# Products of x with w_ch moved between the last group's chunks, and three weight loads cut unevenly

## The chip, the cores and the metric

The kernel runs on one core of a Trainium2 chip. The time is the device time of one execution in microseconds (us). Before the change it is 436.24 us, the median of three runs (435.94 to 436.3 us).

A core has five engines that run beside each other: TensorE (PE: matrix products; PEld is its loading of weights), VectorE (DVE), ScalarE (ACT), GpSimd (POOL) and SyncE (SP). PE writes only to the accumulation memory PSUM, which DVE and ACT read. Sixteen DMA engines move data between the main memory and the on-chip memory.

## The reference

Two layers follow one another. The first is a causal attention with 8 batches, 8 heads, 576 positions and 64 columns a head, and a bias from running sums of `s`. Its result, with the heads side by side, is `x` (8 x 576 x 512). The second mixes along the positions by frequency:

```python
X = np.fft.rfft(x, axis=1)
Xr, Xi = np.real(X[:, :64]), np.imag(X[:, :64])
Yr = einsum('bmd,mde->bme', Xr, w_r) - einsum('bmd,mde->bme', Xi, w_i)
Yi = einsum('bmd,mde->bme', Xr, w_i) + einsum('bmd,mde->bme', Xi, w_r)
y = np.fft.irfft(Y, n=576, axis=1)
u = x + y
out = u + np.maximum(u @ w_ch, 0.0)
```

`w_r` and `w_i` hold a 512 x 512 matrix for each of 64 frequencies: 134 MB in 32-bit numbers, which are read once.

## The kernel before

**Attention.** 32 steps `n` go through 4 groups `g` of two heads and 8 batches. A step computes scores, exponentials and the product with v, leaves its part of `x` in `x_all`, and transforms it to 64 frequencies. The frequency weights of the first three groups (a group is 128 rows of every matrix) are used in between by `quads`, as soon as a group's `x` is complete.

**The weight stream.** Nearly all loads are started by POOL from one list of transfers, by `load` (L311, the start is L315). The weights are asked for in "quarters": `loads_w(upto)` (L294) hands out those up to number `upto`. A unit `u` (`unit_loads`, L249) is 16 frequencies of `w_r` (even `u`) or `w_i` (odd `u`) for one group; there are 24 units of four quarters. A quarter goes to 32 partitions, each of which gets 16 KB of 16-bit numbers (512 KB in all, converted on the way from 1 MB). The last group's weights come as 16 tiles of two transfers each (`tile_loads`, L270): chunk `c` (8 frequencies) has a tile of `w_r` and then one of `w_i`; the last tile comes in four transfers of half size. How far step `n` asks is `on_chip[n]` (L337), a line in `n` that `fits` (L326) cuts where a buffer is still in use. Eight semaphores go round over POOL's transfers, so that the start of one waits until the eighth before it has landed.

**The last group.** After the attention, `modes(NG - 1, c)` (L619) multiplies chunk `c` of the last group: eight matmuls for `w_r`, eight for `w_i` (L628), then POOL's loads that its buffers allow (L645), then an addition of the sum over the other groups on DVE (L651), which gives `yb`. With a `meanwhile`, other work is put in PE's order ahead of one of its four parts (0 and 1 are `w_r`, 2 and 3 `w_i`). `y_transposed` (L839) transposes `yb` on PE (L842) and copies it on ACT (L844). `gather_round` (L857) multiplies transposed chunks with `w_ch` and brings them in order by frequency (L865); its copies (L876) are 16 of 64 rows for chunks 0 to 3 and 16 of 32 rows for chunks 4 and 5, half on ACT and half on DVE.

**Kept products.** The products of `x` with `w_ch` need no frequencies. `work()` (L882) transposes the next pair of blocks of `x` (`x_transposed`, L803: 8 matmuls at L809, two DVE copies at L813) and multiplies the pair before it with `w_ch` (`keep`, L827: 8 matmuls at L822, two ACT copies at L684). Ten calls deal with nine pairs. A tenth pair, `late[-1]`, goes by hand. Pairs 0 and 1 start their product early (`x_times_wch(0, False)`, `x_times_wch(1, False)`) and leave it in PSUM, where the frequency part is added later.

**The order around the change** (L990 to L1049) is Python that is unrolled: each engine carries out its instructions in that order. `TAKE` says how many calls of `work()` chunk `c` gets, `AHEAD` that chunks 0 to 2 may be multiplied one ahead. After chunk 5 stand the transposes of `late[-1]`, 0 and 1, the product of pair 0 and the second round of gathers; chunk 6 has `keep(late[-1])` between its `w_r` and `w_i`; chunk 7 has `first_z(1)` ahead of part 2 and `first_u` ahead of part 3. SP starts a two-number transfer `mark` (L1036) that waits for the last weights, and behind it the transfers `spread` (L662). Then a written list of steps (L1095) ends the work: products, sums and the stores of the result.

Of the kernel before, what the change touches and what calls it, by code (L numbers as in the profile page):

```python
# [19 lines left out]
def kernel(  # L20
# [12 lines left out]
    B, H, S, D = q.shape  # L33
    NM = moe_w_r.shape[0]
    DM = H * D
# [5 lines left out]
    NG = DM // P  # L41
# [6 lines left out]
    NCK = NM // MC  # L48
# [177 lines left out]
    HU = WM * DM  # L226
# [12 lines left out]
    def parts_of(u):  # L239
# [4 lines left out]
            return [(0, ya[:, HU:]), (3, xg[:, 4 * HU : 5 * HU])]  # L244
        return [(0, slot(UNIT_AT[u], 0, 4))]

    wt = {}

    def unit_loads(u):  # L249

        g, c, ri = u // NCK, u % NCK // 2, u % 2
        src = (moe_w_r, moe_w_i)[ri][:, g * P : (g + 1) * P, :]
        slots, todo = [], []
        for j0, t in parts_of(u):
            slots += [t[:, i : i + HU].rearrange("p (q e) -> p q e", q=QD) for i in range(0, t.shape[1], HU)]
        for h in range(QD):
            todo.append([])
            for j0, t in parts_of(u):
                first = 1 if ri == 1 and c + h + j0 == 0 else 0
                j1 = j0 + t.shape[1] // HU  # L260
                todo[-1].append((
                    t[QP * h : QP * h + QP, first * HU :].rearrange("p (j x) -> p j x", x=HU),
                    src[16 * c + 4 * (j0 + first) + h : 16 * c + 4 * j1 - 3 + h : 4].rearrange(
                        "j (p q) e -> p j (q e)", q=QD
                    ),
                ))
        wt[g, c, ri] = slots
        return todo

    def tile_loads(k):  # L270
# [23 lines left out]
    def loads_w(upto):  # L294
        todo = []
        while asked[0] < min(upto, NLW):
            if not queued:
                t = asked[0]
                queued.extend(unit_loads(t // 4) if t < 4 * NUN else tile_loads((t - 4 * NUN) // 2))
            todo += queued.pop(0)  # L300
            asked[0] += 1
        return todo

# [34 lines left out]
    for n in range(N):  # L338
        if n < B:
            w = 4 + (4 * NU + 2) * (n + 1) // (B + 1)  # L340
        else:
            w = 3 * n + 2 if n < 2 * B + 4 else max(59, 4 * n - 22)
        on_chip.append(fits(w, used[n]))


# [273 lines left out]
    def modes(g, c, meanwhile=None, ris=(0, 1)):  # L619


        ps = auxpool.tile([P, DM], FP32, name="yp", tag="aux")
        cols = spectrum(g).rearrange("p q x b m -> p q (x b) m")

        def product(ri, q_, cg):
            k0 = HP if ri == 1 and c == 0 and cg == 0 else 0
            c0 = 2 * B * (1 - ri)
            nc.tensor.matmul(  # L628
                ps[32 * cg : 32 * cg + 32, :],
                cols[k0:, q_, c0 : c0 + 4 * B, 8 * (c // 2) + 2 * cg + c % 2],  # L630
                wt[g, c, ri][cg // 2][k0:, 2 * (cg % 2) + q_, :],
                start=(ri == ris[0] and q_ == 0), stop=(ri == ris[-1] and q_ == 1),
                tile_position=(k0, 32 * cg), skip_group_check=True,
            )

        for x in range(2 * ris[0], 2 * ris[-1] + 2):
            ri, y = divmod(x, 2)
            if meanwhile and x in meanwhile:
                meanwhile[x]()
            for z in range(4):  # L640
                if meanwhile:
                    product(ri, z // 2, 2 * y + z % 2)
                else:
                    product(ri, y, z)
        load(loads_w(fits(NLW, 2 * NUN + 2 * c + ris[-1] + 1)))  # L645
        if ris[-1] == 0:
            nc.vector.tensor_tensor(out=y_acc[:, c, :], in0=ps, in1=y_acc[:, c, :], op=ALU.add)
            return None
        yb = fpool.tile([P, DM], FP16, name="y_sb", tag="y")
        for cols in halves if c == NCK - 1 else [slice(0, DM)]:  # L650
            nc.vector.tensor_tensor(  # L651
                out=yb[:, cols], in0=ps[:, cols], in1=y_acc[:, c, cols], op=ALU.add
            )
        if c >= NCK - 1:
            spread(c, 0, yb)
        return yb
# [146 lines left out]
    def x_transposed(i):  # L803
        xts[i] = xt_sb[len(xts) % 3]
        for x, (b, T) in enumerate(pairs[i]):
            ps = upool.tile([P, DT, P], FP32, name="xt_ps", tag="u")
            for rows, bb, ident in parts(b, T):
                for dt in range(DT):
                    nc.tensor.matmul(  # L809
                        ps[:, dt, rows], x_all[: rows.stop - rows.start, dt, bb, T, :],  # L810
                        ident, start=True, stop=True, skip_group_check=True,
                    )
            nc.vector.tensor_copy(out=xts[i][:, x], in_=ps)  # L813
# [25 lines left out]
    def y_transposed(yb, c=NCK):  # L839
        ps = auxpool.tile([P, DT, P], FP16, name="yt_ps", tag="aux")  # L840
        for dt in range(DT):
            nc.tensor.transpose(ps[:, dt, :], yb[:, bass.ts(dt, P)], ident16h)  # L842
        yt = yt_first[:, :, c % NY, :] if c < NCK - 2 else spool.tile([P, DT, P], FP16, name="yt_sb", tag="yt")
        nc.scalar.copy(out=yt, in_=ps)  # L844
        return yt
# [47 lines left out]

    late = [i for i in kept if i not in first_pairs]
    order_z = late[:-1]
    TAKE = (2, 2, 3, 0, 0, 0)
    us, rs = {}, {}
    last = len(pairs) - 1
    x_pool = ()
# [87 lines left out]
    def z_of(i):  # L987
        return [zs[i, x] for x in range(2)]

    AHEAD = 3  # L990
    ybs = {}
    work()
    for c in range(NCK - 2):
        for x in (c, c + 1):
            if x not in ybs and (x == c or x < AHEAD):
                ybs[x] = modes(NG - 1, x)
        yb = ybs[c]
        for x in range(TAKE[c] - 1):
            work()
        if c == NCK - 3:  # L1000
            x_transposed(late[-1])
            x_transposed(0)
        yt = y_transposed(yb, c)
        if TAKE[c]:
            work()
        if c >= NY:
            if c == NCK - 3:
                x_times_wch(0, False)
                x_transposed(1)
                for which, pool in ((1, auxpool), (0, upool)):  # L1010
                    for x in range(2):
                        gather_round(NY, NCK - 2, 4 * x, which, pool)("sv"[x])
        elif c == NY - 1:
            modes(NG - 1, NY, ris=(0,))
            for x, pool in enumerate((auxpool, upool, auxpool, auxpool)):
                if x == 2:
                    ybs[NY] = modes(NG - 1, NY, ris=(1,))
                for which in (1, 0):
                    gather_round(0, NY, 2 * x, which, pool)()
                if x >= 2:  # L1020
                    work()
    assert not order_z and not ahead
    c = NCK - 2
    yb6 = modes(NG - 1, c, {2: lambda: keep(late[-1])})
    x_times_wch(1, False, (0,))
    yt = y_transposed(yb6)
    x_times_wch(1, False, (1,))
    vb6 = y_times_wch(c, yt)


    def first_u():
# [107 lines left out]
```

## Time and profile before

| what | value |
|---|---|
| profiled execution, its own time | 437.91 us |
| its span, first to last instruction | 436.1 us |
| median of three runs | 436.24 us |
| PE, DVE, ACT, POOL busy | 87%, 59%, 57%, 31% of the span |
| moved by DMA | 92.87 MB as written, 213 GB/s in the mean |
| last weights landed | 400.12 us |
| last product of the last chunk (L628) | starts at 401.61 us, takes 0.65 us |

The profiled execution took 1.67 us more than the median of the runs, and its span 0.14 us less. Times "at" below are from the span's start. "Busy" of PE is modelled for matmuls that overlap. The line `DMA` of the 40 slices is the mean busy share of the sixteen engines; `PEclk` is the granted clock of TensorE. A row of the timeline gives start, duration, engine, line, operation, names and shape, the number of merged instructions, and in brackets the idle time before them and what ended it.

### The profile page before, as it was taken

The page shows a single profiled execution, that of the slowest core. Times are in us where ns is not written, and L with a number is a line of the kernel's source. Part 1 is how long each engine was busy: PE and PEld are TensorE (multiplying, and loading weights), DVE is VectorE, ACT ScalarE, POOL GpSimd, SP SyncE. Part 2 cuts the span into 40 slices and gives each one's busy share as a digit, 9 for nine tenths or more (in the row PEclk, how much of TensorE's full clock was granted, in tenths as well). Part 3 has the DMA queues.
Part 4 walks back from the last instruction along what each step waited for, and adds up shares of the span by engine and source line. Part 5 has one row for each costly group of instructions (what it writes and reads, how often), then busy time and mean ns, then how long its engine had stood idle before and what let it go on. Part 6 is the DMA issues. An engine that isn't in the chain of part 4 may idle for free. (4 is left out here: it accounts for less than half of the span.)

```text
span 436.1 us, 12627 instructions
## 1 busy us (share of the span) xinstructions
PE 381.2 (87%) x5395; PEld 220.2 (50%) x5395; DVE 256.8 (59%) x574; ACT 249.3 (57%) x556; POOL 136.4 (31%) x218
## 2 busy tenths in 40 slices
PE   1599999989999999999997889969885797788994
PEld 1256666645666655656654445535552354443441
DVE  7555666537766765677565566634643255563795
ACT  1377777725866855767774446536540243451894
POOL 6463243131333222323322222222222222210582
PEclk9999999999999999999999799999998799989998
DMA  8999999999999999999999999999999999994598
GB/s 161 208 210 209 213 207 208 213 214 211 212 208 211 210 210 214 210 211 207 210 210 214 212 211 213 210 214 214 212 210 211 212 211 211 211 208 84 202 366 323
DMA packets 47105, 92.87 MB, mean 213 GB/s; under 512 B 8222, under 2 KB 17946, under 8 KB 47050
## 3 DMA queue, kind: packets, MB, share of 16 engines
q0 software_dynamic: 40400, 81.28, 99.1%
q1 hardware_dynamic: 6650, 10.80, 7.1%
q8 instruction: 42, 0.69, 0.6%
q14 instruction: 13, 0.11, 0.1%
HBM read 163.29 MB, written 9.51 MB: 396 GB/s over the span
## 5 line engine op out<-in xcount | busy, mean ns | idle before, releaser
L513 ACT ACTIVATE p_sb<-sc_ps,cumt_sb 128x320 f16<-128x320 f32 (+1 forms) x384 | 161.0, 519 | 33.6 <-PE sc_ps L504 33.6
L504 PE MATMUL sc_ps<-qt,kt 128*64 128x256 bf16 (+3 forms) x640 | 95.4, 294 | 2.0 <-ACT kt L458 1.4
L504 PEld LDWEIGHTS <-kt 128*128 128x128 bf16 (+1 forms) x640 | 50.5, 126 | 62.7 <-issue 36.1
L315 POOL DMA_DIRECT2D w_sb<-in_moe_w_i_dram x62 | 35.2, 567 | 90.7 <-DMA w_sb<-in_moe_w_r_dram 36.5
L458 DVE COPY qt<-tr_ps 64x576 bf16<-64x576 bf16 x64 | 47.7, 745 | 19.6 <-PE tr_ps L454 19.3
L315 POOL DMA_DIRECT2D w_sb<-in_moe_w_r_dram x60 | 34.0, 567 | 76.8 <-DMA w_sb<-in_moe_w_r_dram 28.3
L550 DVE RECIPROCAL rcp<-av_ps 128x5 f32<-128x5 f32 x64 | 12.4, 193 | 75.9 <-PE av_ps L545 75.8
L493 PE MATMUL sc_ps<-negm,ident 128*128 128x512 bf16 x128 | 51.4, 401 | 0.0
L475 ACT ACTIVATE p<-sc_ps,cumt 128x64 f16<-128x64 f32 x32 | 10.1, 314 | 57.3 <-PE sc_ps L471 57.3
L545 PEld LDWEIGHTS <-p_sb 128*128 128x128 f16 x1088 | 40.4, 98 | 3.5
L454 PE MATMUL tr_ps<-ident,qk 64*64 64x64 bf16 x1152 | 31.6, 198 | 10.9 <-DVE kt L458 5.2
L458 ACT COPY kt<-tr_ps 64x576 bf16<-64x576 bf16 x32 | 22.9, 716 | 23.5 <-DVE qt L458 22.9
L454 PEld LDWEIGHTS <-qk 64*64 64x64 bf16 x1152 | 24.2, 111 | 23.7 <-DVE kt L458 8.3
L496 PE MATMUL sc_ps<-negm,ident 128*128 128x256 bf16 x128 | 36.1, 282 | 0.0
L605 PE MATMUL yp<-w_sb,xs 64*32 64x512 bf16 (+1 forms) x704 | 30.6, 403 | 5.0 <-DMA w_sb<-in_moe_w_i_dram 2.4
L545 PE MATMUL av_ps<-va,p_sb 128*128 128x65 f16 x768 | 34.7, 193 | 0.0
L551 DVE TENSOR_TENSOR x_all<-av_ps,rcp 128x320 f16<-128x320 f32 x64 | 31.5, 492 | 2.2
L617 DVE TENSOR_TENSOR y_acc<-yp,y_acc 128x512 f32<-128x512 f32 x34 | 21.9, 686 | 16.9 <-PE yp L605 16.9
L545 PE MATMUL av_ps<-vb,p_sb 128*128 128x65 f16 x320 | 25.8, 195 | 0.0
L315 POOL DMA_DIRECT2D vr<-in_v_dram x22 | 15.1, 688 | 30.4 <-DMA w_sb<-in_moe_w_i_dram 9.9
L458 DVE COPY kt<-tr_ps 64x576 bf16<-64x576 bf16 x32 | 24.4, 763 | 0.4
L605 PEld LDWEIGHTS <-xs 64*32 64x32 bf16 (+1 forms) x768 | 16.2, 139 | 15.5 <-issue 8.0
(127 smaller groups left out, 537.9 us busy)
## 6 DMA issues: line engine op xcount, KB each, us to landing
w_sb<-in_moe_w_r_dram POOLq DMA_DIRECT2D x60, 512.0 KB, 17.1
w_sb<-in_moe_w_i_dram POOLq DMA_DIRECT2D x55, 512.0 KB, 16.7
out_dram<-w_sb SPq DMA_DIRECT2D x16, 512.0 KB
qk<-in_q_dram POOLq DMA_DIRECT2D x15, 288.0 KB, 13.2
qk<-in_k_dram POOLq DMA_DIRECT2D x15, 288.0 KB, 15.0
vr<-in_v_dram POOLq DMA_DIRECT2D x14, 256.0 KB, 15.3
x_all<-in_moe_w_r_dram POOLq DMA_DIRECT2D x4, 512.0 KB, 9.8
y_acc<-in_moe_w_i_dram POOLq DMA_DIRECT2D x3, 384.0 KB, 8.1
```

Source lines behind the costliest of these rows:

```text
L315: nc.gpsimd.dma_start(out=dst, in_=src)
L454: nc.tensor.transpose(ps[rows, r, :], src[rows, r, :], ident16[rows, rows])
L458: copy(out=to[:, :, :, half * RH : half * RH + RH], in_=ps[HP * i : HP * i + HP].rearrange("d r (h p) -> d h p r", h=2),)
L493: nc.tensor.matmul(ps[:, : 2 * W], ident16, both, start=True, stop=False, skip_group_check=True)
L496: nc.tensor.matmul(ps[:, S : S + W], ident16, negm[:, NMB + m0 : NMB + m0 + W], start=True, stop=False, skip_group_check=True,)
L504: nc.tensor.matmul(ps[rows, c0 : c0 + i1 - i0], keys, qh[:, i0:i1], start=False, stop=True, skip_group_check=True,)
L513: nc.scalar.activation(out=pt[:, o : o + n_], in_=ps[:, c0 : c0 + n_], func=ACTF.Exp, bias=cumt_sb[:, x, pidx : pidx + 1], scale=0.125,)
L545: nc.tensor.matmul(ps[:, I, :NCH], lhsT, rhs, start=(i == 0), stop=(i == len(todo) - 1), skip_group_check=True,)
L550: nc.vector.reciprocal(out=rcp, in_=ps[:, :, D])
L551: nc.vector.tensor_tensor(out=x_all[:, g, b, :, D * h : D * h + D], in0=ps[:, :, :D], in1=rcp.unsqueeze(2).to_broadcast([P, NT, D]), op=AL ...
L605: nc.tensor.matmul(ps[hp][32 * j : 32 * j + 32, :], cols[k0:k1, q_, c0 : c0 + 4 * B, 4 * c + j], wt[g, c, ri][j][k0:k1, q_, :], start=(ri ...
L617: nc.vector.tensor_tensor(out=y, in0=ps[hp], in1=y, op=ALU.add)
```

## The change

Two things change. The first is the weight stream. In units 9, 11 and 13 the second quarter no longer goes as one transfer of 32 partitions. It goes as one of 16 partitions and four of eight partitions, which hold, by a partition's 16 KB: all of it (partitions 16 to 23), a sixteenth, three quarters, and three sixteenths (partitions 24 to 31). The four are put in a list `pieces`, and one of them follows each second quarter that is handed out. From step 8 on each step asks one quarter further. The bytes are the same; there are 211 transfers from POOL for 199.

The second is the order in the last group. The loop with `TAKE` and `AHEAD` is replaced by straight code: calls of `work()` stand between `w_r` and `w_i` of chunks 1, 2 and 3 and between the chunks; the transpose of pair 0 goes into the first gathers; one half of pair 0's product, the transpose of `late[-1]` and the transpose of chunk 4 go between `w_r` and `w_i` of chunk 5; and chunk 6's product with `w_ch` (`y_times_wch`) goes ahead of the second half of pair 1's product. The number of calls and the work in each are the same.

```diff
+    ONE_HALF = (9, 11, 13)
+    pieces = []
...
         wt[g, c, ri] = slots
+        if u in ONE_HALF:
+            (dst, src), = todo[1]
+            todo[1] = []
+            for i, (p0, p1, j0, j1, x0, x1) in enumerate((
+                (0, 16, 0, 4, 0, HU), (16, 24, 0, 4, 0, HU), (24, 32, 3, 4, 0, DM), (24, 32, 0, 3, 0, HU),
+                (24, 32, 3, 4, DM, HU),
+            )):
+                (pieces if i else todo[1]).append((dst[p0:p1, j0:j1, x0:x1], src[p0:p1, j0:j1, x0:x1]))
         return todo
...
             todo += queued.pop(0)
+            if asked[0] % 2:
+                todo += pieces[:1]
+                del pieces[:1]
             asked[0] += 1
...
-            w = 3 * n + 2 if n < 2 * B + 4 else max(59, 4 * n - 22)
+            w = 3 * n + 3 if n < 2 * B + 4 else max(60, 4 * n - 21)
...
-    AHEAD = 3
     ybs = {}
     work()
-    for c in range(NCK - 2):
-        for x in (c, c + 1):
-            if x not in ybs and (x == c or x < AHEAD):
-                ybs[x] = modes(NG - 1, x)
-        yb = ybs[c]
-        for x in range(TAKE[c] - 1):
+    ybs[0] = modes(NG - 1, 0)
+    work()
+    ybs[1] = modes(NG - 1, 1, {2: work})
+    work()
+    for x in range(2):
+        y_transposed(ybs[x], x)
+    ybs[2] = modes(NG - 1, 2, {2: work})
+    work()
+    y_transposed(ybs[2], 2)
+    work()
+    ybs[3] = modes(NG - 1, 3, {2: work})
+    work()
+    y_transposed(ybs[3], 3)
+    modes(NG - 1, NY, ris=(0,))
+    for x, pool in enumerate((auxpool, upool, auxpool, auxpool)):
+        if x == 2:
             work()
-        if c == NCK - 3:
-            x_transposed(late[-1])
+            ybs[NY] = modes(NG - 1, NY, ris=(1,))
+        for which in (1, 0):
+            gather_round(0, NY, 2 * x, which, pool)()
+        if x == 2:
             x_transposed(0)
...
-                x_times_wch(0, False)
-                x_transposed(1)
-                for which, pool in ((1, auxpool), (0, upool)):
-                    for x in range(2):
-                        gather_round(NY, NCK - 2, 4 * x, which, pool)("sv"[x])
...
+    def between_5():
+        x_times_wch(0, False, (0,))
+        x_transposed(late[-1])
+        y_transposed(ybs[NY], NY)
+
+    yb = modes(NG - 1, NY + 1, {2: between_5})
+    x_transposed(1)
+    x_times_wch(0, False, (1,))
+    y_transposed(yb, NY + 1)
+    for which, pool in ((1, auxpool), (0, upool)):
+        for x in range(2):
+            gather_round(NY, NCK - 2, 4 * x, which, pool)("sv"[x])
...
     yt = y_transposed(yb6)
+    vb6 = y_times_wch(c, yt)
     x_times_wch(1, False, (1,))
-    vb6 = y_times_wch(c, yt)
```

More of the change, by code (lines that the diff above doesn't have):

```diff
@@ L895 @@
     order_z = late[:-1]
-    TAKE = (2, 2, 3, 0, 0, 0)
     us, rs = {}, {}
@@ L988, in z_of @@
         return [zs[i, x] for x in range(2)]
-    AHEAD = 3
     ybs = {}
     work()
-    for c in range(NCK - 2):
-        for x in (c, c + 1):
-            if x not in ybs and (x == c or x < AHEAD):
-                ybs[x] = modes(NG - 1, x)
-        yb = ybs[c]
-        for x in range(TAKE[c] - 1):
+    ybs[0] = modes(NG - 1, 0)
[14 more added lines that the diff above has]
+        if x == 2:
             work()
-        if c == NCK - 3:
-            x_transposed(late[-1])
+            ybs[NY] = modes(NG - 1, NY, ris=(1,))
+        for which in (1, 0):
+            gather_round(0, NY, 2 * x, which, pool)()
+        if x == 2:
             x_transposed(0)
[L1003 to L1007, printed above, removed]
-                x_times_wch(0, False)
-                x_transposed(1)
-                for which, pool in ((1, auxpool), (0, upool)):
-                    for x in range(2):
-                        gather_round(NY, NCK - 2, 4 * x, which, pool)("sv"[x])
[L1013 to L1021, printed above, removed]
-    assert not order_z and not ahead
+    assert not order_z and not ahead
+    def between_5():
[9 more added lines that the diff above has]
+            gather_round(NY, NCK - 2, 4 * x, which, pool)("sv"[x])
     c = NCK - 2
```

## The prediction

> **What bounds the kernel now.** First the page: the 40 slices and the queues.
>
> ```profile
> span 436.1 us, 12627 instructions
> DMA  8999999999999999999999999999999999994598
> q0 software_dynamic: 40400, 81.28, 99.1%
> q8 instruction: 42, 0.69, 0.6%
> ```
>
> The DMA engines are full until slice 36 (392 us): the weight stream sets the pace, and PE's 87% is no bound. Then the waits, and PE's timeline where the stream ends.
>
> ```profile
> POOL w_sb L315 <- DMA w_sb<-in_moe_w_r_dram: 64.8, 35, 3.8
> ...
> 379.10 0.66 PE L628 MATMUL yp<-w_sb,xs 128*32 128x512 bf16 x8 [1.39 <-DMA w_sb<-in_moe_w_i_dram]
> 379.69 0.62 PE L809 MATMUL xt_ps<-ident16h,x_all 128*128 128x128 f16 x8
> ...
> 382.55 3.16 PE L822 MATMUL z_ps<-wch_sb,xs 128*128 128x512 f16 x8
> 385.65 0.64 PE L809 MATMUL xt_ps<-ident16h,x_all 64*128 64x64 f16 x16
> 386.22 1.95 PE L865 MATMUL g_ps<-wch_sb,yt_first 128*32 128x512 f16 x32
> ...
> 389.75 0.67 PE L628 MATMUL yp<-w_sb,xs 128*32 128x512 bf16 x8 [1.09 <-ACT yv L876]
> 390.35 1.90 PE L822 MATMUL z_ps<-wch_sb,xs 128*128 128x512 f16 x8
> ...
> 388.22 5.60 DVE L876 CAST yv<-g_ps 32x512 f16<-32x512 f32 x8 [0.84 <-PE g_ps L865]
> 393.86 0.69 DVE L651 TENSOR_TENSOR y_sb<-yp,y_acc 128x512 f16<-128x512 f32 x1
> ...
> 401.61 0.65 PE L628 MATMUL yp<-w_sb,xs 128*32 128x512 bf16 x4
> ```
>
> POOL starts a transfer when the eighth before it has landed, so the stream never runs dry. At 379.10 PE waits for chunk 5's last weights (landed 379.05): up to there PE has time to spare. From there to 401.61 it is never again stopped by a landing: chunk 6's weights landed at 384.03 and 389.00, chunk 7's at 395.41, 397.65 and 400.12, and PE comes to them at 389.75, 392.18, 398.03, 399.62, 401.61. Its chain is pair 0's product (3.16 us, at a granted clock of 0.5 from 381.7 to 385.1; the same eight take 1.90 elsewhere), the gathers, their copies on DVE until 393.82, and chunk 6's addition right behind them. So the last stage is 1.5 us later than the last landing alone would make it, and two things have to be earlier: the landings and this chain. What follows 402.26 (33.84 us to the span's end) is PE, ACT and DVE work that starts from the last product.
>
> **Part one: the cut quarters.** Each DMA engine raises a transfer's semaphore once, and the trace holds these sixteen times. For the last transfer they are 392.03, 392.10, 392.25, 392.78, 393.25, 394.29, 394.64, 395.95 and, after a gap, 397.32, 397.44, 397.79, 398.17, 398.45, 398.74, 398.77, 400.12. Eight engines are early, eight late, and a transfer has landed with the latest. The late eight are those that also fetch instructions: after each of the last eight fetches before the end (16 KB, one engine's 0.97 us; at 293.0, 308.0, 315.5, 326.1, 345.5, 363.0, 379.9, 393.2) one time among ranks 9 to 16 falls back by 0.9 to 1.4 us, none among the first eight.
>
> A quarter takes 2.46 us for two partitions an engine, 1.23 each. If a transfer of eight partitions uses eight engines, and the next such transfer the other eight, one group gets 1 + 1 + 0.75 = 2.75 partitions of the quarter and the other 1 + 1/16 + 3/16 = 1.25, for two each: 0.75 x 1.23 = 0.92 us moved a unit, 2.76 in three. The trace of before has no such transfer, so this is unknown between +2.76 and -2.76 for the late eight (0 if all sixteen share). I take relief of the late eight. [...]
> [...]
>
> Twelve more transfers: 16 increments each, 12 x 22 ns (the usual 4-byte packet) = 0.26 at most, or by the smallest loads in the trace (64 KB of v: 0.47 us between two landings for 0.31 by size) 12 x 0.16 = 2.0 us. Below nothing isn't possible: bytes are the same. I take 0.2, the increments, since these rows' 512-byte packets are slow in themselves and the pieces keep packets of 1 to 4 KB. Starting them costs POOL 12 x 0.57 = 6.8 us of issue; POOL is busy 31% and starts transfers eight ahead. The least that seven transfers ahead hold is 8 us in the new order (around step 21; 11 before), of which the spread of the engines takes up to 5: enough.
>
> New landings: early eight + 2.96, late eight - 2.56, the later counts. Last transfer: 395.95 + 2.96 = 398.9 against 397.6: 398.9. Chunk 7's others: 396.4 and 393.9. Chunk 6's last: 388.9. Chunk 5's last: 376.02 + 2.96 = 379.0. The gain (1.2 us) shows only after the fetch at 393.2, and the late eight no longer set it.
>
> One quarter further a step, and the pieces behind, move q and k behind weights: `qk18` lands 2.8 us later (167.4 before, PE transposes it at 167.75), `qk30` 1.7. PE gives it back at unit 23, where it waited 1.62 us, and in 4.01 us at 339.3: nothing at the end; its price uncovered would be up to 1.7.
>
> **Part two: the order.** Until 379.0 PE does the same work plus what is moved ahead: half of pair 0's product (0.95), two transposes (1.26). By rows it is at chunk 5's `w_r` at 374.1 (landing), done with `between_5` at 376.8, and waits 2.2 us. Cost nothing; the cover is the waits (4.01, 1.74, 0.80, 0.48, 1.41) since 339. From 379.0: L628 0.66, transpose of pair 1 and half a product 1.5, transpose of chunk 5 from 381.1, ACT copy 0.6, gathers at 382.3 (before 386.22). Behind them by the old distances: chunk 6's `w_r` 3.5 later at 385.8, `keep` to 388.3, `w_i` at 389.0 (landing), DVE's copies until 382.3 + 7.6 = 389.9, the addition there (before 393.86: 3.9 earlier). Chunk 6's product with `w_ch` follows; the half product now behind it costs 0.4 ahead of `first_z(0)`. Part 3 of chunk 7 could then start at 398.4. But the clock dropped at 381.7 behind a stretch in which PE mostly waited, and 2.2 us of waiting stay here: I keep the half clock, now over the gathers. It adds 1.4 (2.8 us at half): 399.8, later than the landing at 398.9.
>
> **Sum.** End of the last product 399.8 + 0.65 = 400.45 for 402.26: 1.8 us. The tail follows unchanged: its first transfers (`mark`, `spread`) start 1.2 us earlier behind the landing, and what reads chunk 6's rows comes 4 us behind them. Span 434.3, profiled time 436.1, median **434.4**. Without the drop the landing decides: 398.9 + 0.65, gain 2.7, 433.5. Own range 433.2 to 435.3.
>
> **Rivals.**
> 1. The extra load falls on the late eight (the other side). The same trade with the sign turned: last landing 400.12 + 2.76 + 0.2 = 403.1, last product ends 403.75, 1.5 later: **437.7**. The end is later than before once more than 1.3 us go to them. For it: nothing in the trace numbers the engines. [...]
> 2. It doesn't shift: the small transfers are shared by all sixteen or land alike on both groups. Landing 400.3, end 400.95, **434.9**: the order alone.
> 3. Small transfers pay as the 64 KB ones: landing 398.7 + 2.0 = 400.7, end 401.35, **435.3**. [...]
> 4. The clock drops to half in the tail, where PE is busy 27 of 34 us: 3.4 us at half add 1.7: **436.1**. Before, the next drop came at 432.9, past PE's last work.
>
> **How the numbers follow.** Forecast 0.55, rivals 0.20, 0.10, 0.07, 0.08. A measurement of this kernel tells 0.2%, 0.87 us, from no change. Faster: 0.52 + 0.10 + 0.03 = 0.65. Slower: rival 1 and a little of 4 = 0.24. Same 0.11. The range goes from the forecast's lower end, 433.2, up over rival 1 to 437.8, since without it too much is left out.
>
> **What would show it.** The sixteen times of the last transfer closer together than 8.1 us (right: about 6; rival 1: over 10). PE's wait for chunk 5's `w_i` of about 2 us, at 379. Gathers near 382 for 386.2, chunk 6's addition near 390 to 391. A wait for DMA ahead of the last L628, or a half clock across the gathers: which of the two bounds decides. Wrong: chunk 5's last weights landing at 381 or later, or PE coming to them late.

## The result and the profile after

The changed kernel is slower: a median of 439.98 us (six runs, 438.86 to 442.63) against 436.09 us of the kernel before (six runs, 434.95 to 436.65), a ratio of 1.0100 with a 95% interval of 1.0082 to 1.0118. The prediction was 434.4 us, with a range from 433.2 to 437.8. The profiled execution took 440.14 us, its span is 438.0 us.

From the page of the changed kernel: the span, the busy share of the DMA engines and what they moved in the 40 slices, and two queues.

```profile
span 438.0 us, 12646 instructions
...
DMA  9999999999999999999999999999999999996798
GB/s 166 207 209 211 211 209 209 213 213 211 211 212 195 212 181 211 202 194 201 203 210 214 212 204 212 210 213 214 213 210 212 211 211 211 211 212 114 220 367 319
...
q0 software_dynamic: 40832, 81.28, 100.4%
...
q8 instruction: 42, 0.69, 0.6%
```

The DMA engines stay busy further into slice 37 (0.6 of it for 0.4), yet queue q0 moves the same 81.28 MB. So the time went into the stream itself. The rates say where: 209 to 214 GB/s in most slices, but 195, 181, 202, 194, 201 and 203 in six of the slices 13 to 20 (131 to 219 us), where units 9, 11 and 13 are loaded. The last transfer's sixteen times, which the prediction had expected to end at 398.9, are

```
before 392.03 392.10 392.25 392.78 393.25 394.29 394.64 395.95 397.32 397.44 397.79 398.17 398.45 398.74 398.77 400.12
after  396.19 396.37 396.89 397.38 398.11 400.70 400.81 401.11 401.23 401.33 401.74 401.88 402.19 402.69 402.80 403.20
```

All sixteen engines are later: the mean goes from 395.9 to 400.3, by 4.4 us, and the last from 400.12 to 403.20. PE's timeline of the changed kernel at the end of the stream (start, duration, engine, line, operation; in brackets the idle time before it and what ended it):

```profile
382.90 0.66 PE L641 MATMUL yp<-w_sb,xs 128*32 128x512 bf16 x8 [1.87 <-DMA w_sb<-in_moe_w_i_dram]
...
386.06 1.95 PE L878 MATMUL g_ps<-wch_sb,yt_first 128*32 128x512 f16 x32 [0.73 <-ACT yt_first L857]
...
389.60 0.67 PE L641 MATMUL yp<-w_sb,xs 128*32 128x512 bf16 x8 [1.09 <-ACT yv L889]
...
392.85 0.67 PE L641 MATMUL yp<-w_sb,xs 128*32 128x512 bf16 x8 [0.75 <-DMA w_sb<-in_moe_w_i_dram]
...
400.75 0.65 PE L641 MATMUL yp<-w_sb,xs 128*32 128x512 bf16 x4 [0.75 <-DMA w_sb<-in_moe_w_i_dram]
...
403.24 0.65 PE L641 MATMUL yp<-w_sb,xs 128*32 128x512 bf16 x4 [0.43 <-DMA w_sb<-in_moe_w_i_dram]
```

L641 is the L628 of before, and L878 the L865. PE now waits for landings four times, the last time directly ahead of the last product. So that product ends at 403.89, where it ended at 402.26, and 0.69 behind the last landing instead of 2.14. What lies behind it, 34.1 us, is what it was (33.84).

The same stretch, 130 to 220 us, in the view of the DMA engines, each figure the rate of one of 40 parts of 2.25 us. Before:

```profile
GB/s 209 213 207 213 216 204 210 210 210 212 205 214 204 211 216 214 214 215 205 220 208 210 212 210 210 213 209 207 217 211 211 207 204 209 206 211 209 204 217 212
DMA packets 9552, 18.94 MB, mean 210 GB/s; under 512 B 2161, under 2 KB 4781, under 8 KB 9538
...
q0 software_dynamic: 9494, 18.71, 111.0%
```

And after:

```profile
GB/s 208 153 200 211 205 216 221 202 208 217 204 202 198 147 154 210 211 208 214 211 171 214 209 210 212 172 177 205 204 206 208 174 215 206 208 194 190 209 209 214
DMA packets 9525, 18.02 MB, mean 200 GB/s; under 512 B 2656, under 2 KB 4933, under 8 KB 9512
...
q0 software_dynamic: 9476, 17.81, 113.4%
```

There are three pits after, around 132, 160 to 163 and 188 us (and lesser ones around 175 and 201), and 18.02 MB are moved in place of 18.94. The 0.92 MB that are missing take 4.4 us at 0.21 MB/us, as much as all engines are late by. The engines were not idle meanwhile: the weight queue's packets filled a larger share of their time (113.4% for 111.0%; above 100% the packets' times overlap). Each packet took longer. A packet of 4,096 bytes usually takes 324 ns; between 158 and 164 us its mean was 457 ns.

For comparing the runs, a measure from the trace's packets: **the excess packet time** is what the weight queue's packets took above what is usual for their size (324 ns for 4,096 bytes, 192 for 2,304, 173 for 2,048, 98 for 1,024, 60 for 512, 32 for 128, 22 for 4, the most frequent values; a packet that took less counts as nothing), added up and divided by sixteen. It is 2.2 us for each engine before and 9.5 after; 7.2 of the 9.5 lie between 130 and 220 us.

### The profile page after: what moved, and what is told of

Read it like the earlier page. It is cut to its first block, busy times and chain, and to the rows that moved or that the text cites. A ratio compares the mean times of both kernels' runs of the same rounds, so it can differ in the third digit from the quotient of the medians.

```text
span 438.0 us, 12646 instructions
## 1 busy us (share of the span) xinstructions
PE 383.6 (88%) x5395; PEld 221.2 (51%) x5395; DVE 256.9 (59%) x574; ACT 249.3 (57%) x556; POOL 143.1 (33%) x230
## 3 DMA queue, kind: packets, MB, share of 16 engines
q0 software_dynamic: 40832, 81.28, 100.4%
## 5 line engine op out<-in xcount | busy, mean ns | idle before, releaser
L328 POOL DMA_DIRECT2D w_sb<-in_moe_w_i_dram x74 | 41.9, 566 | 101.2 <-DMA w_sb<-in_moe_w_r_dram 41.5
L697 ACT COPY w_sb<-z_ps 128x512 f32<-128x512 f32 x20 | 11.7, 587 | 21.7 <-PE z_ps L716 15.2
```

What stands on the lines that cost most here:

```text
L328: nc.gpsimd.dma_start(out=dst, in_=src)
```

## The experiments

Times are medians; "last" and "mean" are the last and the mean of the last transfer's sixteen times, "excess" is the measure above, all three from the profiled execution. The two kernels with two quarters in eights ran on another chip, where the kernel before took 437.57 us in its one run beside them.

| kernel | time, us (runs) | ratio to before, 95% | last | mean | excess |
|---|---|---|---|---|---|
| before | 436.09 (6) | | 400.12 | 395.9 | 2.2 |
| changed | 439.98 (6) | 1.0100 (1.0082 to 1.0118) | 403.20 | 400.3 | 9.5 |
| order alone | 436.13 (11) | 0.9998 (0.9984 to 1.0012) | 399.71 | 395.7 | 1.9 |
| cut alone | 440.32 (6) | 1.0093 (1.0073 to 1.0113) | 403.25 | 399.5 | 7.6 |
| cut by every second row | 436.53 (12) | 1.0012 (0.9997 to 1.0028) | 399.14 | 396.5 | 2.7 |
| the same, sizes exchanged | 437.05 (10) | 1.0016 (0.9999 to 1.0034) | 399.61 | 396.6 | 2.7 |
| two halves of neighbours | 438.79 (1) | | 402.04 | 399.3 | 7.1 |
| two halves, every second | 436.52 (10) | 1.0016 (0.9992 to 1.0040) | 398.86 | 395.8 | 2.1 |
| neighbours, six units | 443.38 (4) | 1.0175 (1.0136 to 1.0215) | 407.08 | 403.4 | 14.5 |
| near rows, far partitions | 439.40 (1) | | 399.38 | 396.5 | 2.9 |
| far rows, near partitions | 440.05 (1) | | 403.21 | 400.1 | 8.7 |
| before, once more | 435.74 (1) | | 398.72 | 395.4 | 1.7 |
| two quarters in eights, 32 apart | 444.55 (1) | | 407.92 | 404.6 | 12.9 |
| two quarters in eights, 48 or 16 apart | 441.11 (1) | | 404.44 | 401.4 | 7.8 |

### One part at a time

The order alone: the changed kernel without any cut quarter.

```diff
-    ONE_HALF = (9, 11, 13)
+    ONE_HALF = ()
```

> The new order of the last group and the one quarter more a step, with no quarter cut. If the order did what the prediction says and the loss is all in the cut quarters: last weights land at 400 to 400.6 us as before, the last L628 product ends 0.7 us behind them (2.1 before), POOL's queue keeps 99% of the engines' time, 434.3 to 435.0 us. If part of the loss is in the order or in asking a quarter further: 436 or more.

The cut alone: the kernel before with `ONE_HALF`, `pieces` and the new steps of the weights, and its own order in the last group.

```diff
-            w = 3 * n + 2 if n < 2 * B + 4 else max(59, 4 * n - 22)
+            w = 3 * n + 3 if n < 2 * B + 4 else max(60, 4 * n - 21)
...
+    ONE_HALF = (9, 11, 13)
```

> The cut quarters and the one quarter more a step, with the old order of the last group. If the loss is all in the cut quarters: the DMA rate falls below 205 GB/s in the slices between 130 and 220 us, last weights land at 402.5 to 404, and behind them the old order takes its 1.5 to 2.1 us: 439 to 441.5 us, slower than both parts together. If the two parts only hurt together: 435.5 to 437.

The order alone takes 436.13 us, the kernel before in the same session 436.23 (23 runs): no difference that can be measured, and not the 434.3 to 435.0 us that were expected of it; the last of these sections says why. The cut alone takes 440.32, so it costs 4.1 us and is the whole of the loss. Its view of the DMA engines from 130 to 220 us has the same pits:

```profile
GB/s 209 183 193 211 206 221 208 207 210 218 205 204 203 129 155 201 213 205 220 210 202 213 216 208 210 172 178 212 200 211 209 206 210 210 204 189 196 211 204 212
DMA packets 9650, 18.19 MB, mean 202 GB/s; under 512 B 2660, under 2 KB 5026, under 8 KB 9638
```

### What the cut does to the packets

The pieces, by every second partition and row of the quarter: first the even ones, then the odd ones of the lower half, then those of the upper half in the three sizes.

```diff
-                (0, 16, 0, 4, 0, HU), (16, 24, 0, 4, 0, HU), (24, 32, 3, 4, 0, DM), ...
+                (slice(0, 32, 2), slice(0, 32, 2), 0, 4, 0, HU),
+                (slice(1, 16, 2), slice(1, 16, 2), 0, 4, 0, HU),
+                (slice(17, 32, 2), slice(17, 32, 2), 3, 4, 0, DM),
...
```

> As the change, but the quarter is cut by even and odd partitions: sixteen even ones in one transfer, the odd ones below 16 in place of 16 to 23, the odd ones above 16 in place of 24 to 31. [...] If the slow packets come from engines that meet in the same stretch of the weights or of the partitions: no burst in the transfers of sixteen, at most the shorter ones of the three-quarter transfers (0.5 us each); last weights at 398.5 to 400.5, 433.3 to 435 us. If small transfers are slow in themselves: bursts as in the change, 438 or more.

As many transfers, of the same sizes, with the same bytes, and the pits are gone:

```profile
GB/s 208 213 203 212 209 214 213 208 211 212 205 214 210 208 218 216 208 211 208 220 212 210 212 211 201 213 211 211 207 211 205 210 215 201 193 209 213 208 206 219
DMA packets 10058, 18.90 MB, mean 210 GB/s; under 512 B 2690, under 2 KB 5294, under 8 KB 10045
```

18.90 MB where the changed kernel moved 18.02, and 436.53 us. So it is neither the number of the transfers nor their size that makes the pits, but which rows and partitions they hold. Quite free the twelve are not: the mean of the sixteen times is 396.5 to 396.6 in the three kernels that have them without neighbours in their partitions, and 395.4 to 395.9 in the four with neither pieces nor slow packets (before, twice; order alone; two halves, every second). The last time is no later (399.1 to 399.6 against 398.7 to 400.1). The other way round, without any transfer of eight: the quarter as two halves of sixteen neighbours.

```diff
+                (slice(0, 16), slice(0, 16), 0, 4, 0, HU),
+                (slice(16, 32), slice(16, 32), 0, 4, 0, HU),
```

> As the change, but the three quarters go as two transfers of sixteen neighbouring partitions each and none of eight, so that no load moves between engines. If sixteen neighbouring partitions on sixteen engines make the slow packets: six bursts, DMA rate under 205 GB/s between 130 and 220 us, last weights at 402 to 406. If the transfers of eight make them: no burst, last weights at 400 to 400.8, the gap between the early and the late engines as before, 434.3 to 435.2 us.

And its counterpart, in which only the distance differs.

```diff
+                (slice(0, 32, 2), slice(0, 32, 2), 0, 4, 0, HU),
+                (slice(1, 32, 2), slice(1, 32, 2), 0, 4, 0, HU),
```

> The three quarters each as two transfers of 16 partitions, but of every second partition and row (the even ones, then the odd ones), with the new order; nothing goes as eight. Against the run with two halves of 16 neighbouring partitions (excess packet time 7.1 us for each engine, last weights at 402.0, 438.8 us) only the distance of the partitions differs. Theory 'neighbouring partitions written by several engines at once make packets slow': excess 1.7 to 2.8 us, slices 206 to 214 GB/s, last landing 398.7 to 400, time 435.7 to 436.7. Rival 'any transfer of fewer than 32 partitions does': excess 6 to 8 us, last landing 401.5 to 403, time 438 to 440.

The two views from 130 to 220 us, neighbours first:

```profile
GB/s 212 173 171 202 212 214 208 204 221 203 207 219 208 144 155 153 187 211 211 218 215 208 211 214 220 199 207 208 209 216 209 215 213 210 204 206 203 221 203 214
DMA packets 9271, 18.31 MB, mean 203 GB/s; under 512 B 2305, under 2 KB 4616, under 8 KB 9258
```

```profile
GB/s 208 207 206 213 210 220 206 203 225 201 211 212 211 210 213 217 211 214 211 215 214 212 217 203 210 211 211 203 214 218 207 209 211 197 212 218 202 212 206 217
DMA packets 9693, 18.97 MB, mean 211 GB/s; under 512 B 2333, under 2 KB 4915, under 8 KB 9679
```

With neighbours 18.31 MB, pits down to 144 GB/s and an excess of 7.1 us; by every second one 18.97 MB, no pit, and 2.1 us. From 160 to 165 us the packets of 4,096 bytes took 520 ns in the mean with neighbours. The rival, that any transfer of fewer than 32 partitions is slow, falls. Not every cut quarter has its pit: the two halves of unit 13 (about 188 us) have none here, and why is open.

Then the same in six units in place of three.

```diff
-    ONE_HALF = (9, 11, 13)
+    ONE_HALF = (5, 7, 9, 11, 13, 15)
```

> Two halves of 16 neighbouring partitions in six units (5, 7, 9, 11, 13 and 15) where it was three, with the new order. Theory 'each such quarter costs its own slow packets': twice the 4.9 to 5.4 us of excess that three quarters had over the order alone (7.13 against 1.89), so excess 11 to 13 us, slow slices at six places between 60 and 230 us, last landing 404 to 406, time 440.5 to 443. Rival 'once some engines are out of step, what is slow does not depend on how many quarters are cut': excess 6 to 8.5 us, last landing 401.5 to 403.5, time 438 to 440.

From 80 to 230 us (3.75 us for each figure), six units, and below it the order alone:

```profile
GB/s 186 128 197 209 212 216 212 211 190 193 194 212 210 207 209 152 213 213 205 213 207 213 163 153 205 217 213 210 214 207 210 209 214 213 210 203 210 164 202 186
DMA packets 14595, 30.02 MB, mean 200 GB/s; under 512 B 3309, under 2 KB 6956, under 8 KB 14572
```

```profile
GB/s 212 213 215 213 213 211 216 204 208 214 214 211 207 206 211 214 211 206 213 209 216 209 215 214 212 212 214 208 211 211 213 211 216 201 213 205 211 210 206 211
DMA packets 15374, 31.65 MB, mean 211 GB/s; under 512 B 3272, under 2 KB 7402, under 8 KB 15350
```

The loss grows with the number of cut quarters. There are five stretches of pits for the six units; at the place of unit 13 (about 188 us) there is none here either. 31.65 - 30.02 = 1.63 MB are missing, 7.7 us at 0.211 MB/us. The excess is 14.5 us, and the time 443.38. That is more than the expected 11 to 13 us and 440.5 to 443, and the rival, a loss that does not depend on the number, is out.

### Reading or writing

A transfer of neighbours reads neighbouring rows of DRAM and writes neighbouring partitions of SBUF. Two kernels part the two: the near rows into every second partition,

```diff
+                (slice(0, 32, 2), slice(0, 16), 0, 4, 0, HU),
+                (slice(1, 16, 2), slice(16, 24), 0, 4, 0, HU),
...
```

> The new order, with the quarter cut as in the change in its rows of DRAM (16 neighbouring rows, then 8 and 8), but written to every second partition of the quarter's 32. So the weights of that quarter stand in other partitions than they should, and the products use wrong rows; the instructions, bytes and waits are those of the change. Theory A (reads: engines that read 16 neighbouring rows of DRAM at once get in each other's way): the slow packets stay, excess packet time about 7 to 9.5 us for each engine as in the changed kernel, slices of 180 to 202 GB/s between 131 and 205 us, the last weights land at 402 to 403.5. Theory B (writes: neighbouring partitions of SBUF get in each other's way): no such slices (206 to 213 GB/s), excess 2 to 3 us, last landing 399 to 400. Theory C (reads and writes both have to lie apart): as A here and in the next run too.

and every second row into near partitions.

```diff
+                (slice(0, 16), slice(0, 32, 2), 0, 4, 0, HU),
+                (slice(16, 24), slice(1, 16, 2), 0, 4, 0, HU),
...
```

> The mirror of the run before: every second row of DRAM is read, and 16 neighbouring partitions are written (then 8 and 8); again the rows stand in the wrong partitions and the products use wrong rows. Theory A (reads): no slow slices, excess 2 to 3 us, last landing 399 to 400, span 434 to 435.5. Theory B (writes): excess 7 to 9.5 us, slices of 180 to 202 GB/s between 131 and 205 us, last landing 402 to 403.5, span 437 to 438.5. Theory C: as B here, and as A in the run before. If neither run shows the slow slices, what counts is that a row and its partition are shifted by nothing against each other, which neither theory has.

Near rows and far partitions, then far rows and near partitions:

```profile
GB/s 210 209 203 213 207 217 211 203 217 211 204 214 212 208 217 214 211 209 215 219 205 211 213 213 206 208 216 198 218 209 206 212 209 197 198 210 211 213 208 216
DMA packets 10060, 18.90 MB, mean 210 GB/s; under 512 B 2691, under 2 KB 5295, under 8 KB 10047
```

```profile
GB/s 210 166 177 199 210 206 220 208 209 208 213 205 217 165 157 184 213 202 212 214 211 207 219 202 220 197 153 217 199 207 210 208 196 214 208 207 193 213 208 212
DMA packets 9631, 18.22 MB, mean 202 GB/s; under 512 B 2690, under 2 KB 4992, under 8 KB 9619
```

It is the writing: with the partitions apart there is no pit (18.90 MB, excess 2.9 us, last landing 399.38), with neighbouring partitions there are all of them (18.22 MB, 8.7, 403.21), whatever is read. Theory B had both runs. The first took 439.40 us although its weights were there at 399.38, for another reason:

```profile
383.54 3.64 PE L881 MATMUL g_ps<-wch_sb,yt_first 128*32 128x512 f16 x32 [0.73 <-ACT yt_first L860]
...
402.53 0.65 PE L644 MATMUL yp<-w_sb,xs 128*32 128x512 bf16 x4
```

Its gathers (L881, 1.95 us in the changed kernel) took 3.64 at a granted clock of 0.54 between 384 and 388 us, and the last product came at 402.53, not behind a landing. The clock was at half twice in this chain, from 380.9 to 387.7 us and from 394.5 to 397.9. This is the half clock across the gathers, which the prediction had named, and it is not rare: of the five profiled executions with the new order and without slow packets, three have it, with gathers of 3.64 us here, 3.64 with the sizes exchanged and 3.41 in the two halves at every second partition.

### Neighbours or partitions 32 apart

In the pit of the run with two halves (160 to 165 us) the middle packet of 4,096 bytes took 526 ns, for the usual 324, and one in ten over 605. Whether it takes neighbours for that shows where no transfer writes neighbouring partitions. Here the first two quarters of the three units go as eights of every second partition, in turn, one of the first quarter and then one of the second, whose partitions lie 32 above.

```diff
+            r = [slice(0, 16, 2), slice(1, 16, 2), slice(16, 32, 2), slice(17, 32, 2)]
+            for i, (a, b) in enumerate(((0, 0), (1, 1), (2, 2), (3, 3))):
+                todo[i // 2] += [(d0[r[a]], s0[r[a]]), (d1[r[b]], s1[r[b]])]
```

> In units 9, 11 and 13 the first two quarters (partitions 0 to 31 and 32 to 63) go as eights of every second partition, one quarter's eight and the other quarter's in turn, so that while one group of eight engines writes partitions 0, 2, ... 14 (then 1, 3, ... 15) the other writes 32, 34, ... 46 (then 33, ... 47), and so on for the upper halves. No transfer writes neighbouring partitions. Theory 'adjacency' (only neighbouring partitions make packets slow): excess packet time 2 to 3.5 us for each engine, no slow slices between 130 and 205 us, as in the next run. [...]

The control has `((0, 2), (1, 3), (2, 0), (3, 1))` in the second line: the two of a pair lie 48 partitions apart, or 16. That 32 apart would be the slower of the two was the author's assumption.

> The control to the run before: the same sixteen... eight-partition transfers in each unit by count and size, but the second quarter's halves change places, so that while one group writes 0, 2, ... 14 the other writes 48, 50, ... 62. [...] If small transfers as such make the stream run dry or slow, both runs show it alike, with last landings over 401 in both.

32 apart, then 48 or 16 apart:

```profile
GB/s 198 143 117 160 198 214 209 208 210 213 208 219 192 143 143 153 113 197 206 209 226 207 209 216 208 170 168 186 122 172 200 214 215 208 214 213 214 198 202 209
DMA packets 9653, 17.15 MB, mean 191 GB/s; under 512 B 3229, under 2 KB 5296, under 8 KB 9640
```

```profile
GB/s 208 159 125 171 195 215 207 202 215 213 214 215 200 190 162 136 213 211 215 217 208 216 209 212 208 203 187 197 189 218 213 207 216 216 201 210 198 215 207 205
DMA packets 10057, 18.04 MB, mean 200 GB/s; under 512 B 3266, under 2 KB 5453, under 8 KB 10044
```

No transfer writes neighbouring partitions, and the run with 32 apart has the deepest pits of all, down to 113 GB/s: excess 12.9 us, against the 2 to 3.5 that adjacency alone would give. Against the control it has 5.0 us more excess and lands 3.5 us later. From 160 to 165 us the packets of 4,096 bytes took 587 ns in the mean, in the control 452. But the control is not clean: it has an excess of 7.8 us itself where adjacency alone would give 2 to 3.5 as well, and both dip at 132 to 137 us (to 117 and 125 GB/s), where eights follow each other. Both also land later than 401 (407.92 and 404.44), which was named as the sign that small transfers as such are slow. Twelve such pieces at every second partition made no pit, but eights that follow each other directly were tried in these two runs alone. Which engines each eight went to they do not show. So it is shown that writing neighbouring partitions is what slows the packets in the changed kernel (excess 8.7 us with neighbours in the partitions, 2.9 with neighbours in the rows alone), and that it isn't necessary for slow packets (12.9 and 7.8 us without). That the distance of the partitions counts, 32 for 48 or 16, rests on one execution of each, and what it is in these two runs that slows the packets was not shown.

### Which engines the eights relieve

The cut by every second row again, with the large and the small pieces exchanged in the order of issue.

```diff
-                (slice(1, 16, 2), slice(1, 16, 2), 0, 4, 0, HU),
-                (slice(17, 32, 2), slice(17, 32, 2), 3, 4, 0, DM),
+                (slice(17, 32, 2), slice(17, 32, 2), 3, 4, 0, DM),
+                (slice(1, 16, 2), slice(1, 16, 2), 0, 4, 0, HU),
...
```

> The cut by every second row (no slow packets there), new order, but the large and the small pieces change places in the order of issue, so that the eight engines that were relieved now get 2.76 us more than an even share instead of less. Theory 'a group of eight is really shifted': last weights land about 2 to 3.5 us after those of the order alone (399.7), at 401.5 to 403, spread of the sixteen times 9.5 to 11 us, time 437.5 to 439.5. Rival 'the groups of eight do not decide which engines are late': last landing 399 to 400, time 436.0 to 437.0.

The last landing moves by 0.47 us, from 399.14 to 399.61, and the spread of the sixteen times from 6.7 to 6.8. The time of 437.05 us is just above the rival's 437.0; its profiled execution (439.31 us) has the half clock across the gathers. If a group of eight had been shifted by 2.76 us one way and then the other, it would have been seen.

The sixteen times of the transfers in unit 9 say why in part. A piece with all the bytes of its eight partitions (a whole piece) does go to eight engines: it moves eight of the times by 1.24 to 1.26 us and the other eight by 0.16 to 0.18. That is a fit to the times ahead of it and behind it, off by 0.01 to 0.03 us in the mean in the three kernels with pieces at every second partition, where a shift that is the same for all sixteen is off by 0.22 to 0.32. But the next piece need not go to the other eight. With the sizes exchanged, the packets of 1,024 bytes end with ranks 2, 3, 5, 6, 7, 9, 10 and 12 (within 0.04 us, against the sixteen times of two transfers before), and the whole piece behind them moves just these ranks. If two pieces in a row use the same engines, exchanging them changes nothing. With the sizes exchanged the fit puts the three-quarter pieces (0.75 of the bytes of eight partitions) mostly on the other eight. A reading from that, not settled, is that one group gets 1 + 1 + 1/16 + 3/16 = 2.25 partitions of the quarter and the other 1.75, in either order: 0.31 us a unit and not 0.92.

Nor is a group the early eight or the late eight. In the changed kernel the packets of 1,024 bytes end with ranks 3, 5, 6 and 12 to 16 of the sixteen times in unit 9, and much the same in units 11 and 13. Each group holds early engines and late ones, so a trade between the groups cannot bring the late ones down without raising others of them.

### Why the order gains nothing

The kernel before, unchanged, in another profiled execution.

> The kernel before once more, with a profile, since the order alone left the time where it was (436.13 against 436.23) although the profiled execution of before had its last product end at 402.26 and that of the order alone at 400.40. Theory D (the profiled execution of before was a late one by its own 0.95 of the clock between 381.7 and 385.1, in front of the gathers): here the products before the gathers take 1.9 us and not 3.16, gathers at 385.0 or earlier, last product ends at 400.6 to 401.3, own time 435.8 to 436.5. Rival E (the chain ends as late as then, and the order gives the gain back in the tail): gathers at 386 or later, last product ends at 402 or later, and the rest of the kernel after it is under 33.9 us, half a microsecond or more below the 34.46 us of the order alone.

Its timeline at the end of the stream, and below it that of the order alone:

```profile
381.60 1.90 PE L822 MATMUL z_ps<-wch_sb,xs 128*128 128x512 f16 x8
...
384.00 1.95 PE L865 MATMUL g_ps<-wch_sb,yt_first 128*32 128x512 f16 x32
...
397.40 0.65 PE L628 MATMUL yp<-w_sb,xs 128*32 128x512 bf16 x4
...
399.38 0.65 PE L628 MATMUL yp<-w_sb,xs 128*32 128x512 bf16 x4
```

```profile
378.96 0.67 PE L641 MATMUL yp<-w_sb,xs 128*32 128x512 bf16 x8 [0.64 <-DMA w_sb<-in_moe_w_i_dram]
...
382.12 1.95 PE L878 MATMUL g_ps<-wch_sb,yt_first 128*32 128x512 f16 x32 [0.73 <-ACT yt_first L857]
...
397.29 0.65 PE L641 MATMUL yp<-w_sb,xs 128*32 128x512 bf16 x4 [0.77 <-DMA w_sb<-in_moe_w_i_dram]
...
399.75 0.65 PE L641 MATMUL yp<-w_sb,xs 128*32 128x512 bf16 x4 [0.41 <-DMA w_sb<-in_moe_w_i_dram]
```

Before, with the full clock, pair 0's product takes 1.90 us where the profiled execution of the prediction had 3.16, the gathers start at 384.00 and the last product at 399.38, 0.66 behind the last landing (398.72), without waiting for it. With the new order the gathers start at 382.12 and the last product at 399.75, 0.04 behind its landing (399.71). So all that the order can save is about 0.6 us of 436, 0.14%, which 34 runs do not tell from nothing. From the last landing to the span's end it was 35.2 us here, and 34.7 to 35.2 in the eight profiled executions of the new order whose gathers ran at full clock. What differs between these two ends is the landing, 1.0 us, and that differs between executions of the kernel before as well (398.72 and 400.12). Theory D had it, though the granted clock between 381.7 and 385.1 had been 0.50 and not the 0.95 that its text gives; the last product ended even earlier than expected, at 400.03.

Against that stands the half clock. In the three executions of the new order that have it across the gathers, the way from the last landing to the end was 36.0, 37.6 and 37.9 us. The run times have such a tail too: of the 43 runs of the four kernels with the new order and without slow packets that ran more than once, ten took longer than 437.68 us, the longest of the 48 runs of the kernel before beside them. That these ten had the half clock there is likely, but only one of them (439.31 us) was profiled.

## Why the prediction was wrong

**The step that failed** is in part one: the twelve small transfers "I take 0.2, the increments", with the reason that "the pieces keep packets of 1 to 4 KB", and a bound of 2.0. The working asked how many bytes each engine gets, how small the packets are and what a transfer costs at its start. It did not ask where in SBUF sixteen engines write at the same time, and carried the 1.23 us for a partition over from the uncut quarters to the pieces. The transfer of sixteen partitions was costed at nothing. Two of these to a quarter, without any eights, have an excess of 5.2 us above the order alone in three units (7.1 against 1.9). In the changed kernel it was 7.6 us above the order alone (9.5 against 1.9), the sixteen times' mean came 4.4 us later than before, and the cut alone took 4.1 us more. The 398.9 for the last landing became 403.20, and "chunk 5's last weights landing at 381 or later", named as the sign that the prediction is wrong, came true (the wait ended at 382.90).

**The shift of 2.76 us** to the early engines was not seen either. The sixteen times' spread went from 8.1 to 7.0 us, where 6 was expected; but the kernel before has 6.8 in its other execution, and two halves without eights have 6.9. With the order of the pieces exchanged nothing changed. Two assumptions failed: that the next such transfer goes to the other eight engines (with the sizes exchanged two in a row used the same eight), and that a group of eight is the early eight or the late eight. That the late eight would be the ones relieved, by 2.76 us, was the author's choice, and no run shows it: the runs show eight of the times moved by 1.24 to 1.26 us by a whole piece, and the eight that took the packets of 1,024 bytes in the changed kernel's unit 9 were ranks 3, 5, 6 and 12 to 16, early and late mixed.

**Rival 1**, the load on the late eight, has the right sign and nearly the right landing (403.1 for 403.20), but not the mechanism: it asked for a spread over 10 us, and the spread shrank. All engines were late, by slower packets (457 ns for 324 between 158 and 164 us), so that the landing agrees is luck. **Rival 2**, the order alone, was to take 434.9 us, and the order alone took 436.13: its gain is part two's, of which more below. **Rival 3**, small transfers that pay as those of 64 KB do (0.16 us each), had the place (the cut) and neither size nor mechanism: in the run times the same twelve by every second row cost nothing that can be told from zero (1.0012, interval 0.9997 to 1.0028). In the mean of the sixteen times they cost 0.6 to 1.2 us, more than the 0.2 that was taken: there are 408 more packets of 4 bytes and not 192, and the eight engines that get no row of a piece still lose 0.16 to 0.18 us by it. **Rival 4** did not come: in the changed kernel's profiled execution the clock next dropped at 435.9 us, behind PE's last work.

**Part two** was right in its mechanism. The order alone starts the gathers at 382.12 (expected 382.3), adds chunk 6 at 389.75 on DVE (389.9) and ends the last product at 400.40 (400.45), though with the landing as the bound and without the half clock that was forecast, so that the end agrees to 0.05 us is luck. Even in the changed kernel the wait ahead of chunk 5's `w_i` was 1.87 us (expected 2.2), only at 382.90 instead of 379, and the addition came no earlier than before:

```profile
393.70 0.69 DVE L664 TENSOR_TENSOR y_sb<-yp,y_acc 128x512 f16<-128x512 f32 x1
```

Its gain was mis-sized: 1.8 us were taken off against an execution that carried a half clock in just this chain. The prediction saw the drop, put it into the changed kernel too, and then took the difference off the median, although that execution took 1.67 us more than the median. Against an execution at full clock, 0.6 us was there to be had.

**The rest held.** The tail behind the last product was 33.8 to 34.5 us in all profiled executions (34.5 with the order alone). Handing out weights one quarter further cost nothing at the end: the order alone has it and takes the time of before. The half clock across the gathers came in three profiled executions of the new order, not in those of the changed kernel or the order alone.

## What to carry to other kernels

Before a transfer is cut, ask which partitions the engines will write at the same moment: three quarters cut into pieces of neighbouring partitions cost about 1% of this kernel, and cut the same way by every second partition nothing that the run times show. Every second partition is no safeguard by itself, as the two runs with two quarters in eights tell (12.9 and 7.8 us of excess). When the weight stream sets the pace, look at the rate in slices of a few microseconds and at the packets' durations; a queue that is full can be full of slow packets (100.4% of the span here, for 99.1% before). And a gain that is read from one profiled execution is only as good as that execution: look for a lowered clock in the very chain that is to be shortened, and set it against a second one.

## What the runs showed of the hardware

- Sixteen neighbouring partitions written by sixteen engines: 4,096-byte packets of 520 ns in the mean for 324 (160 to 165 us, two halves), rates down to 144 GB/s for 211. By every second partition: 324 ns in the mean from 158 to 167 us.
- Reading neighbouring rows did no harm: 18.90 MB in the 90 us with near rows and far partitions, for 18.94 of before.
- The slow packets are not only those of the cut transfers: between 160 and 163 us those of 2,304 bytes, from the loads of q and k that were not cut, take 299 ns in the mean for 192 in the changed kernel, and between 130 and 136 us those of 128 bytes 47 ns for 32.
- A transfer of eight partitions moves eight of the sixteen times by 1.24 to 1.26 us and the other eight by 0.16 to 0.18 (unit 9, the three kernels with pieces at every second partition).
- Between 250 and 270 us, during the load of `w_ch` with its 128 partitions, five of the six kernels with `pieces` of eight have an excess of 0.8 to 1.2 us (the cut alone 0.3), the two with two quarters in eights 0.1 and 0.3, and those without eights 0.06 to 0.4. Nothing was tried on it.
